# Late weight tiles of a dense layer: decode steps moved between the products and the low half, in the order of use

## The chip, the core and the metric

The kernel runs on one core of a Trainium2 chip. The metric is device time in microseconds (us), the median of several runs of the same compiled kernel. PE is TensorE, DVE is VectorE, ACT is ScalarE, POOL is GpSimd, SP is SyncE.

## The reference, cut to what matters

An attention-like recurrence gives x (3072 tokens of 384), a mixture of experts maps it to x again, and a gated dense layer ends the chain. Only the dense layer is touched:

```
g = x @ w_gate                     # 384 -> 1536
silu = g * (1.0 / (1.0 + np.exp(-g)))
val = x @ w_val                    # 384 -> 1536
return (silu * val @ w_out)        # 1536 -> 384
```

The three weight matrices of the dense layer reach the kernel as float64 bit patterns.

## The kernel before

**Two halves of a float.** Each fp32 operand of a matmul is split in a high part (a cast to fp32r on ACT) and a low part (source minus high part, on DVE); a product is three matmuls, high by high, high by low and low by high. `split` (L1431) issues the two instructions.

**The dense loop.** The tokens are in 8 blocks of 384, the hidden width in 12 parts f of 128. `seq` (L1568) runs block by block over the parts: 96 steps, numbered n, so steps 0 to 11 are the first block. A step issues `up2(j, f)` (L1521): 9 matmuls into the PSUM tile pg, 9 into pv, the sigmoid on ACT (L1532), two products on DVE (L1533 reads pg, L1534 reads pv, both write sg), then `split` of sg into the tiles hd, the high half by a cast on ACT (L1432), the low half on DVE (L1433). Two steps later `down2` (L1541) issues the 9 matmuls into po that read hd. There are two pg and two pv tiles, so the pg matmuls of step n+2 wait until L1533 of step n has read its pg. The engines run in the order in which the code issues, since the schedule is written out by hand.

**The weights.** Each part needs three weight tiles of 128 by 384: number m = 3f (gate), 3f+1 (val), 3f+2 (out), 36 in all. The first 30 (`NDEC`) are decoded from float64 during the mixture of experts and lie in fp32. In the dense loop `split_w2(n + 2)` (L1459) splits the three tiles of part n+2, ahead of `up2` of step n: three casts on ACT, three subtractions on DVE. That goes on through step 7.

**The six late tiles** (30 to 35, of parts 10 and 11) are decoded inside the first steps. `decode_parts` (L1252) gives five DVE instructions per tile: L1268 shifts, L1270 merges, L1272 takes the exponent, L1273 scales the low word, L1263 adds the two; after the last, `load_raw` (L1291) starts on POOL's queue the transfer of the tile three places on, into one of three rawd buffers. `decode_late` (L1450) adds a sixth part, `f_split`: cast on ACT and, right behind it, the subtraction on DVE that needs it. After `up2`, steps 0 to 7 take 5, 4, 5, 4, 5, 4, 5, 4 of these 36 parts (L1576 to 1582), tile by tile from 30 to 35. Parts 10 and 11 are used from steps 10 and 11 on, tiles 32 and 35 (out) first in steps 12 and 13.

Of the kernel before, what the change touches and what calls it, by code (L numbers as in the profile page):

```python
# [10 lines left out]
F32 = mybir.dt.float32  # L11
# [5 lines left out]
ALU = mybir.AluOpType  # L17
# [172 lines left out]
def tile_kernel(  # L190
# [8 lines left out]
    ve, sc, gp, pe, sy = nc.vector, nc.scalar, nc.gpsimd, nc.tensor, nc.sync  # L199
# [5 lines left out]
    P = 128  # L205
    NC_ = S // P
    NTILE = NT // P
    G3 = DM // P
    D2 = 2 * D
    KF1 = F1 // P  # L210
    KF2 = F2 // P
# [134 lines left out]
    for r in range(2):  # L346
# [7 lines left out]
        p=(1, WIDE), r=(1, WIDE), tw=(1, WIDE), ta=(1, WIDE), tr=(1, [P, CM, H, 2, D]),  # L354
# [793 lines left out]
    with tc.If(slow > 0):  # L1148
# [14 lines left out]
        with tc.For_i(0, S, TS) as t0:  # L1163
            tl = {}
            for nm, src in (("ar", a_re), ("ai", a_im), ("q", q), ("k", k)):
                t = slowp.tile([P, TS, D], F32, name="f" + nm)
# [8 lines left out]
            w = slowp.tile([P, TS, D], F32, name="fw")  # L1175
# [69 lines left out]
    NW = 3 * KF2  # L1245

    NDEC = NW - 6
    wls = ctx.enter_context(tc.tile_pool(name="wls", bufs=NDEC, reuse_waits="tile"))
    wf = [wls.tile([P, G3, P], F32, name="w") for m in range(NDEC)]
    raws = []  # L1250

    def decode_parts(m, w):  # L1252
        def raw():
            return raws[m % 3]

        def hw():
            return w().bitcast(I32)

        def hi():
            return raw()[:, :, :, 1]  # L1260

        def f_rest():
            ve.tensor_tensor(out=w(), in0=w(), in1=hi().bitcast(F32), op=ALU.add)  # L1263
            if m + 3 < (NDEC if m < NDEC else NW):
                load_raw(m + 3)

        return [
            lambda: ve.tensor_scalar(out=hw(), in0=hi(), scalar1=3, scalar2=0x3FFFFFFF, op0=ALU.logical_shift_left,  # L1268
                                     op1=ALU.bitwise_and),
            lambda: ve.scalar_tensor_tensor(out=hw(), in0=hi(), scalar=-0x40000000, in1=hw(), op0=ALU.bitwise_and,  # L1270
                                            op1=ALU.bitwise_or),
            lambda: ve.tensor_scalar(out=hi(), in0=hw(), scalar1=-0x00800000, scalar2=None, op0=ALU.bitwise_and),  # L1272
            lambda: ve.scalar_tensor_tensor(out=hi().bitcast(F32), in0=raw()[:, :, :, 0].bitcast(U32), scalar=2.0**-52,  # L1273
                                            in1=hi().bitcast(F32), op0=ALU.mult, op1=ALU.mult),
            f_rest,
        ]

    undone, parts = list(range(NDEC)), []

# [8 lines left out]
    decp = dec.enter_context(tc.tile_pool(name="decp", bufs=1, side="right", reuse_waits="tile"))  # L1288
    raws += [decp.tile([P, G3, P, 2], I32, name=f"raw{i}") for i in range(3)]

    def load_raw(m):  # L1291
        raw = raws[m % 3]
        f, i = divmod(m, 3)
        if i == 2:
            gp.dma_start(raw.rearrange("p g f t -> p (g f t)"), w2_out.bitcast(I32)[f * P : (f + 1) * P, :])
        else:
            src = (w2_gate, w2_val)[i].bitcast(I32)[:, f * 2 * P : (f + 1) * 2 * P]
            gp.dma_start(raw.rearrange("p g f t -> p g (f t)"), src.rearrange("(g p) f -> p g f", p=P))

    for m in range(3):  # L1300
        load_raw(m)
# [70 lines left out]
    def slot(s):  # L1372

        for f in range(KF1):
# [19 lines left out]
            step[0] += 1  # L1394
            while done[0] * STEPS < 5 * NDEC * step[0] and (parts or undone):
                if not parts:
# [21 lines left out]
    def den_pool(name, bufs, **kw):  # L1418
        return den.enter_context(tc.tile_pool(name=name, bufs=bufs, reuse_waits="tile", **kw))
# [3 lines left out]

    NEW0, NEW = 4, NW + NW - NDEC + 1
    dsoon = den_pool("dsoon", 1)
# [3 lines left out]
    xb, wd, wnew = {}, {}, [None]  # L1429

    def split(dst, src):  # L1431
        sc.copy(dst[0], src)  # L1432
        ve.tensor_tensor(out=dst[1], in0=src, in1=dst[0].bitcast(F32), op=ALU.subtract)  # L1433

    def prep_g(j, g):
        if j < len(BLKS):
            c, n = BLKS[j]
            xb[j] = xbs[j % 2]
            split([t[:, g, :n] for t in xb[j]], x2T[:, g, SLOT + c : SLOT + c + n])
# [3 lines left out]
    def new_hl():  # L1443
        n_hl[0] += 2
        return [(w0 if n < NEW0 else wnew[0] if n < NEW else wls).tile([P, G3, P], F32R, name="w")
                for n in (n_hl[0] - 2, n_hl[0] - 1)]

    late, late_parts = {}, []

    def decode_late(m):  # L1450
        w = latep.tile([P, G3, P], F32, name="wl")

        def f_split():
            late[m] = new_hl()
            split(late[m], w)

        return decode_parts(m, lambda: w) + [f_split]

    def split_w2(f, n_m=3):  # L1459
        wd.setdefault(f, [])  # L1460
        for m in range(3 * f + len(wd[f]), 3 * f + n_m):
            if m < NDEC:
                hl = new_hl()
                split(hl, wf[m])
            else:
                hl = late.pop(m)
            wd[f].append(hl if m % 3 < 2 else [t.rearrange("p g f -> p (g f)") for t in hl])

    soon_parts = [lambda g=g: prep_g(0, g) for g in range(G3)] + [lambda m=m: split_w2(0, m) for m in (1, 2)]
    slot(NSURE - 1)  # L1470
    assert not undone and not parts
# [34 lines left out]
    latep = den_pool("latep", 2)  # L1506
    raws[:] = [rawp.tile([P, G3, P, 2], I32, name=f"rawd{i}") for i in range(3)]
    for m in range(NDEC, NDEC + 3):
        load_raw(m)
# [8 lines left out]

    hd = {}

    def up2(j, f):  # L1521
        n_ = BLKS[j][1]
        ps = []
        for w, nm in zip(wd[f][:2], "gv"):
            p_ = dp_u.tile([P, BLK], F32, name="p" + nm)[:, :n_]
            xh, xl = xb[j]
            terms = [(a, xh, g) for g in range(G3) for a in w] + [(w[0], xl, g) for g in range(G3)]
            for n, (a, x, g) in enumerate(terms):
                pe.matmul(p_, a[:, g, :], x[:, g, :n_], start=(n == 0), stop=(n == 3 * G3 - 1))  # L1529
            ps.append(p_)  # L1530
        sg = dtwo.tile([P, BLK], F32, name="sg")[:, :n_]
        sc.activation(out=sg, in_=ps[0], func=AF.Sigmoid)  # L1532
        ve.tensor_tensor(out=sg, in0=sg, in1=ps[0], op=ALU.mult)  # L1533
        ve.tensor_tensor(out=sg, in0=sg, in1=ps[1], op=ALU.mult)  # L1534
        hl = [dthr.tile([P, BLK], F32R, name=f"hd{i}")[:, :n_] for i in range(2)]
        split(hl, sg)
        hd[j, f] = hl

    po = {}

    def down2(j, f, ts=range(BLK // P)):  # L1541
        hh, hl = hd[j, f]
        oh_, ol_ = wd[f][2]
        if f == 0:
            po[j] = [dp_o.tile([P, BLK], F32, name=f"po{t}") for t in range(BLKS[j][1] // P)]
        for t in ts:
            p_ = po[j][t]
            sl = slice(t * P, (t + 1) * P)
            for i, (h, w) in enumerate(((hh, oh_), (hh, ol_), (hl, oh_))):
                pe.matmul(p_[:, :DM], h[:, sl], w, start=(f == 0 and i == 0), stop=(f == KF2 - 1 and i == 2))  # L1550

    def write(j, ts=range(BLK // P)):
        for t in ts:
            p_ = po[j][t]
            o = dfou.tile([P, DM], F32, name="o")
            sc.copy(o, p_[:, :DM])  # L1556
            i = BLKS[j][0] // P + t
            d = gp.indirect_dma_start(out=out, out_offset=bass.IndirectOffsetOnAxis(ap=idu[:, i : i + 1], axis=0),  # L1558
                                      in_=o, in_offset=None)
            gp.memset(pause, 0.0)  # L1560

            tc.declare_no_dep(d.ins, group="out", reason="each token number occurs once")
            tc.add_to_no_dep_group("out", d.ins)

    split_w2(0)
    split_w2(1)
    late_done = []
    seq = [(j, f) for j in range(len(BLKS)) for f in range(KF2)]  # L1568
    for n, (j, f) in enumerate(seq):
        if f == KF2 - 2:  # L1570
            for g in range(G3):
                prep_g(j + 1, g)
        if n + 2 < KF2:
            split_w2(n + 2)
        up2(j, f)
        if n < KF2 - 3:  # L1576
            todo_late = -(-6 * (NW - NDEC) * (n + 1) // (KF2 - 4))
            while len(late_done) < min(todo_late, 6 * (NW - NDEC)):
                if not late_parts:
                    late_parts.extend(decode_late(NDEC + len(late_done) // 6))  # L1580
                late_parts.pop(0)()
                late_done.append(n)
        if n == KF2 // 2:
            ve.tensor_copy(idu, idf)

        if 1 < n < len(seq) - 1:
            jp, fp = seq[n - 2]
            down2(jp, fp)
            if fp == KF2 - 1:
                write(jp)  # L1590

    down2(*seq[-3])
    for t in range(BLK // P):
        for jp, fp in seq[-2:]:
            down2(jp, fp, (t,))
        write(len(BLKS) - 1, (t,))
# [34 lines left out]
```

## Time and profile before

| | |
|---|---|
| median of 3 runs | 947.86 us (947.84 to 947.98) |
| the profiled execution's own time | 950.28 us |
| its span, first to last instruction | 948.6 us |
| busy: PE, DVE, ACT, POOL | 904.9, 594.7, 448.9, 120.6 us |
| granted TensorE clock, mean of the span | 0.983 of full speed |

The dense loop begins at 481 us of the span and runs to its end. Times in the rows below count from the start of the span. A matmul of 128 by 384 shows as about 338 ns busy, but the matmuls overlap each other; the time from the first matmul of one step to the first of the next is what counts.

### The profile page before, as it was taken

To read this page: it belongs to the slowest core of one execution; us is meant where nothing else is said; L and a number is where in the kernel's file an instruction comes from. 1 tells how busy PE (TensorE), PEld (TensorE's weight loads), DVE (VectorE), ACT (ScalarE), POOL (GpSimd) and SP (SyncE) were. 2 spreads that over 40 slices of the span, in tenths; PEclk is the share of its full clock that TensorE was granted. 3 is DMA by queue.
4 is the path that set the end of the run, shared out by engine and by line. 5 is a ranking of instruction groups with operands and counts; after the bars stand their busy time and mean duration, and the time that the engine had idled before them with its cause. 6 is when DMAs were issued, how large, how long until landed. Compare 5 with 4: busy or idle time off the path is not lost. (4 is left out here: it accounts for less than half of the span.)

```text
span 948.6 us, 15710 instructions
## 1 busy us (share of the span) xinstructions
PE 904.9 (95%) x5980; PEld 868.9 (92%) x5980; DVE 594.7 (63%) x1147; ACT 448.9 (47%) x775; POOL 120.6 (13%) x210
## 2 busy tenths in 40 slices
PE   2789999999999999999998999999999999999997
PEld 1578889888998999999988899999999999999997
DVE  6999999988666888798778733334343343434332
ACT  6899887788645554545444322222222232222221
POOL 1112423322120101110010010100101000010101
PEclk9789999999998999999999999999999999999999
DMA  9999775683015574432121000000000000000000
GB/s 167 160 185 186 129 135 120 150 196 95 35 60 89 107 178 126 93 80 65 51 68 34 1 26 1 26 1 1 26 1 26 1 9 17 1 26 1 26 1 26
DMA packets 155646, 64.57 MB, mean 68 GB/s; under 512 B 135540, under 2 KB 150188, under 8 KB 155564
## 3 DMA queue, kind: packets, MB, share of 16 engines
q1 hardware_dynamic: 147564, 39.82, 22.8%
q0 software_dynamic: 8000, 23.69, 9.5%
q8 instruction: 48, 0.79, 0.4%
q14 instruction: 34, 0.28, 0.1%
HBM read 67.86 MB, written 14.37 MB: 87 GB/s over the span
## 5 line engine op out<-in xcount | busy, mean ns | idle before, releaser
L1529 PE MATMUL pg<-xb,w 128*128 128x384 f32 x864 | 167.6, 338 | 7.4 <-DVE sg L1533 6.1
L1529 PE MATMUL pv<-xb,w 128*128 128x384 f32 x864 | 167.6, 339 | 0.0
L1550 PE MATMUL po<-w,hd 128*128 128x384 f32 x864 | 165.7, 337 | 0.0
L1529 PEld LDWEIGHTS pg<-xb,w 128*128 128x128 f32 x864 | 152.2, 188 | 9.7 <-DVE sg L1533 8.1
L1533 DVE TENSOR_TENSOR sg<-sg,pg 128x384 f32<-128x384 f32 x96 | 53.1, 553 | 163.9 <-ACT sg L1532 163.9
L1529 PEld LDWEIGHTS pv<-xb,w 128*128 128x128 f32 x864 | 153.5, 191 | 0.0
L1550 PEld LDWEIGHTS po<-w,hd 128*128 128x128 f32 x864 | 151.6, 188 | 0.0
L1432 ACT CAST hd<-sg 128x384 fp32r<-128x384 f32 x96 | 49.3, 513 | 160.7 <-DVE sg L1534 160.7
L1532 ACT ACTIVATE sg<-pg 128x384 f32<-128x384 f32 x96 | 47.2, 491 | 161.6 <-PE pg L1529 161.6
L1433 DVE TENSOR_TENSOR hd<-sg,hd 128x384 fp32r<-128x384 f32 x96 | 53.5, 558 | 55.6 <-ACT hd L1432 51.6
L1534 DVE TENSOR_TENSOR sg<-sg,pv 128x384 f32<-128x384 f32 x96 | 53.2, 554 | 36.5 <-PE pv L1529 35.1
L1558 POOL DMA_INDIRECT out_dram<-o,idu x24 | 23.3, 972 | 408.9 <-ACT o L1556 405.8
L991 ACT ACTIVATE hh<-banks 128x396 fp32r<-128x396 f32 x64 | 32.1, 502 | 84.0 <-PE banks L988 80.5
L988 PE MATMUL banks<-xh,w1h 128*128 128x396 f32 x192 | 67.6, 352 | 1.6 <-DVEq L1238 1.6
L988 PE MATMUL banks<-xh,w1l 128*128 128x396 f32 x192 | 66.8, 348 | 0.0
L995 DVE SCALAR_TENSOR_TENSOR hl<-banks,hh 128x396 fp32r<-128x396 f32 x64 | 36.3, 567 | 34.0 <-ACT hh L991 33.6
L668 PE MATMUL banks<-tQ,tK 96*128 96x128 f32 x384 | 51.3, 279 | 0.0
L668 PEld LDWEIGHTS banks<-tQ,tK 96*128 96x128 f32 x384 | 46.5, 191 | 2.7 <-issue 1.4
L1002 PE MATMUL banks<-hh,w2l 128*128 128x396 f32 x192 | 47.7, 343 | 0.0
L1002 PE MATMUL banks<-hh,w2h 128*128 128x396 f32 x192 | 47.7, 343 | 0.0
L1002 PE MATMUL banks<-hl,w2h 128*128 128x396 f32 x192 | 47.7, 343 | 0.0
L988 PE MATMUL banks<-xl,w1h 128*128 128x396 f32 x192 | 45.9, 348 | 0.0
(217 smaller groups left out, 1533.7 us busy)
## 6 DMA issues: line engine op xcount, KB each, us to landing
st<-in_moe_w_dram SPq DMA_DIRECT2D x64, 384.0 KB
xrows<-zero SPq DMA_DIRECT2D x8, 597.1 KB
xg<-xrows SPq DMA_DIRECT2D x8, 597.1 KB
ar<-in_a_re_dram SPq DMA_DIRECT2D x24, 192.0 KB
ai<-in_a_im_dram SPq DMA_DIRECT2D x24, 192.0 KB
q<-in_q_dram SPq DMA_DIRECT2D x24, 192.0 KB
k<-in_k_dram SPq DMA_DIRECT2D x24, 192.0 KB
v<-in_v_dram SPq DMA_DIRECT2D x24, 192.0 KB
```

What stands on the lines that cost most here:

```text
L668: pe.matmul(plan[ap][:, i * P : (i + 1) * P], plan[kt][:, i, :], plan[qt][:, i, :], start=True, stop=True)
L988: pe.matmul(ps[:, :SLOT], a[:, g, o : o + P], x[:, g, :], start=(n == 0), stop=(n == 3 * G3 - 1))
L991: sc.activation(out=hidden(s, f)[0], in_=ps[:, :SLOT], func=AF.Relu)
L995: ve.scalar_tensor_tensor(out=hl, in0=ps[:, :SLOT], scalar=0.0, in1=hh.bitcast(F32), op0=ALU.max, op1=ALU.subtract)
L1002: pe.matmul(pds[:, g, :SLOT], w[:, f % 2, g * P : (g + 1) * P], x, start=(f == 0 and term == 0), stop=(f == KF1 - 1 and term == 2))
L1432: sc.copy(dst[0], src)
L1433: ve.tensor_tensor(out=dst[1], in0=src, in1=dst[0].bitcast(F32), op=ALU.subtract)
L1529: pe.matmul(p_, a[:, g, :], x[:, g, :n_], start=(n == 0), stop=(n == 3 * G3 - 1))
L1532: sc.activation(out=sg, in_=ps[0], func=AF.Sigmoid)
L1533: ve.tensor_tensor(out=sg, in0=sg, in1=ps[0], op=ALU.mult)
L1534: ve.tensor_tensor(out=sg, in0=sg, in1=ps[1], op=ALU.mult)
L1550: pe.matmul(p_[:, :DM], h[:, sl], w, start=(f == 0 and i == 0), stop=(f == KF2 - 1 and i == 2))
```

## The change

The decode parts of the late tiles are no longer issued behind `up2` but inside it, through a new argument `between`: behind the cast of the high half of hd and ahead of the subtraction that makes its low half. Steps 0 to 7 take three parts each, steps 8 and 9 six each (`N_LATE`; step 10 finds none left). The order of tiles becomes 30, 31, 33, 34, 32, 35 (`TURN_W`), for the transfers too. The sixth part of a tile is taken apart: its cast on ACT goes with the fifth part, its subtraction on DVE becomes the second part of the next tile.

```
+    TURN_W = list(range(NDEC)) + [NW - 6, NW - 5, NW - 3, NW - 2, NW - 4, NW - 1]
...
     def decode_late(m):
-        w = latep.tile([P, G3, P], F32, name="wl")
-
-        def f_split():
+        w = []
+
+        def f_hi():
             late[m] = new_hl()
-            split(late[m], w)
-
-        return decode_parts(m, lambda: w) + [f_split]
+            sc.copy(late[m][0], w[0])
+
+        def f_lo():
+            ve.tensor_tensor(out=late[m][1], in0=w[0], in1=late[m][0].bitcast(F32), op=ALU.subtract)
+
+        parts = decode_parts(m, lambda: w[0])
+        first, last = parts[0], parts[-1]
+        begin = lambda: (w.append(latep.tile([P, G3, P], F32, name="wl")), first())
+        return [begin] + parts[1:-1] + [lambda: (last(), f_hi())], f_lo
...
-    def up2(j, f):
+    def up2(j, f, between=lambda: None):
...
         ve.tensor_tensor(out=sg, in0=sg, in1=ps[1], op=ALU.mult)
         hl = [dthr.tile([P, BLK], F32R, name=f"hd{i}")[:, :n_] for i in range(2)]
-        split(hl, sg)
+        sc.copy(hl[0], sg)
+
+        between()
+        ve.tensor_tensor(out=hl[1], in0=sg, in1=hl[0].bitcast(F32), op=ALU.subtract)
         hd[j, f] = hl
...
-    late_done = []
+
+    for m in TURN_W[NDEC:]:
+        ps_, lo = decode_late(m)
+        if late_parts:
+            ps_.insert(1, late_parts.pop())
+        late_parts += ps_ + [lo]
+    N_LATE = [3] * (KF2 - 4) + [6] * 3 + [0]
+    assert sum(N_LATE) >= len(late_parts)
+
+    def decode_some(n):
+        def f():
+            for part in late_parts[: N_LATE[n]]:
+                part()
+            del late_parts[: N_LATE[n]]
+
+        return f
+
...
-        up2(j, f)
-        if n < KF2 - 3:
-            todo_late = -(-6 * (NW - NDEC) * (n + 1) // (KF2 - 4))
-            while len(late_done) < min(todo_late, 6 * (NW - NDEC)):
-                if not late_parts:
-                    late_parts.extend(decode_late(NDEC + len(late_done) // 6))
-                late_parts.pop(0)()
-                late_done.append(n)
+        up2(j, f, decode_some(n) if j == 0 else lambda: None)
```

The rest of the diff lets `load_raw` and the rawd buffers go by the place in `TURN_W` instead of the tile's number, and lets `up2` and `down2` fetch a part's weights by `w_of`. For the first 30 tiles place and number are the same.

## Rows read from the trace of the kernel before

**Rows 1.** Stretches: length, busy us of each engine (instructions), granted PE clock, DMA share, GB/s.
```profile
core 0: us, PE busy (x) PEld busy (x) DVE busy (x) ACT busy (x) POOL busy (x), PEclk, DMA share, GB/s
487.38:535.78 48.40, 42.25 (x217) 40.29 (x217) 39.47 (x83) 19.44 (x45) 2.05 (x3) 0.93 0.08 25
504.84:511.20 6.36, 6.36 (x27) 6.31 (x28) 4.98 (x11) 2.65 (x6) 0.56 (x1) 0.73 0.07 28
529.42:535.78 6.36, 6.36 (x27) 6.36 (x28) 4.35 (x9) 2.23 (x5) 0.00 (x0) 0.73 0.01 3
540.48:573.32 32.84, 32.84 (x190) 32.84 (x190) 12.27 (x23) 8.69 (x18) 3.34 (x6) 1.00 0.05 18
```

**Rows 2.** Waits, 487 to 536 us: who waited for whom, us, times, longest.
```profile
PE pg L1529 <- DVE sg L1533: 6.1, 6, 1.9
DVE hd L1433 <- ACT hd L1432: 5.2, 9, 0.6
DVE w L1433 <- ACT w L1432: 2.4, 4, 0.6
```

**Rows 3.** Chain that ended last, 491 to 506 us: start, us, what.
```profile
492.20 0.47 DVE sg L1533
...
492.76 0.56 DVE sg L1534
...
493.35 0.52 ACT hd L1432
...
493.90 0.56 DVE hd L1433
494.46 0.47 DVE w L1433
494.93 0.28 DVE wl L1268
...
495.23 0.57 DVE wl L1270
...
495.83 0.36 DVE rawd L1272
496.19 1.40 DVE w L1433 x3
497.59 0.47 DVE sg L1533
...
499.85 0.48 DVE rawd L1273
...
500.36 0.57 DVE wl L1263
...
500.95 0.52 ACT w L1432
...
501.49 0.56 DVE w L1433
...
504.32 0.47 DVE sg L1533
```

**Rows 4.** Order of time on DVE, steps 0 and 1: start, us, instruction, idle before.
```profile
485.99 0.55 DVE L1533 TENSOR_TENSOR sg<-sg,pg 128x384 f32<-128x384 f32 x1 [0.92 <-ACT sg L1532]
...
489.64 0.56 DVE L1273 SCALAR_TENSOR_TENSOR rawd<-rawd 128x384 f32<-128x384 uint32 x1
...
490.71 1.49 DVE L1433 TENSOR_TENSOR w<-w 128x384 fp32r<-128x384 f32 x3
492.11 0.55 DVE L1533 TENSOR_TENSOR sg<-sg,pg 128x384 f32<-128x384 f32 x1
```

**Rows 5.** Stretches of 1 us while the first late tiles land, columns as in rows 1.
```profile
485.00:486.00 1.00, 1.00 (x8) 1.00 (x7) 0.09 (x2) 0.95 (x2) 0.00 (x0) 1.00 1.00 338
487.00:488.00 1.00, 1.00 (x8) 1.00 (x7) 0.42 (x2) 0.76 (x2) 0.00 (x0) 1.00 0.00 0
```

**Rows 6.** Order of time on PE, the two longest waits of the first block.
```profile
504.84 2.00 PE L1529 MATMUL pg<-xb,w 128*128 128x384 f32 x9 [1.77 <-DVE sg L1533]
...
529.42 2.58 PE L1529 MATMUL pg<-xb,w 128*128 128x384 f32 x9 [1.86 <-DVE sg L1533]
```

More of the change, by code (lines that the diff above doesn't have):

```diff
@@ L1252, in decode_parts @@
     def decode_parts(m, w):
+        at = TURN_W.index(m)
         def raw():
-            return raws[m % 3]
+            return raws[at % 3]
         def hw():
@@ L1263, in f_rest @@
             ve.tensor_tensor(out=w(), in0=w(), in1=hi().bitcast(F32), op=ALU.add)
-            if m + 3 < (NDEC if m < NDEC else NW):
-                load_raw(m + 3)
+            if at + 3 < (NDEC if at < NDEC else NW):
+                load_raw(at + 3)
         return [
@@ L1289, in tile_kernel, with load_raw @@
     raws += [decp.tile([P, G3, P, 2], I32, name=f"raw{i}") for i in range(3)]
-    def load_raw(m):
-        raw = raws[m % 3]
-        f, i = divmod(m, 3)
+    def load_raw(at):
+        raw = raws[at % 3]
+        f, i = divmod(TURN_W[at], 3)
         if i == 2:
@@ L1450, in decode_late, with w_of @@
     def decode_late(m):
-        w = latep.tile([P, G3, P], F32, name="wl")
-        def f_split():
+        w = []
+        def f_hi():
             late[m] = new_hl()
-            split(late[m], w)
-        return decode_parts(m, lambda: w) + [f_split]
+            sc.copy(late[m][0], w[0])
[5 more added lines that the diff above has]
+        return [begin] + parts[1:-1] + [lambda: (last(), f_hi())], f_lo
     def split_w2(f, n_m=3):
         wd.setdefault(f, [])
[L1461 to L1467, printed above, removed]
+        for m in range(3 * f + len(wd[f]), min(3 * f + n_m, NDEC)):
+            hl = new_hl()
+            split(hl, wf[m])
+            wd[f].append(hl)
+    def w_of(f, i):
+        hl = wd[f][i] if 3 * f + i < NDEC else late[3 * f + i]
+        return hl if i < 2 else [t.rearrange("p g f -> p (g f)") for t in hl]
     soon_parts = [lambda g=g: prep_g(0, g) for g in range(G3)] + [lambda m=m: split_w2(0, m) for m in (1, 2)]
@@ L1519, in tile_kernel @@
     hd = {}
-    def up2(j, f):
+    def up2(j, f, between=lambda: None):
         n_ = BLKS[j][1]
         ps = []
-        for w, nm in zip(wd[f][:2], "gv"):
+        for w, nm in zip((w_of(f, 0), w_of(f, 1)), "gv"):
             p_ = dp_u.tile([P, BLK], F32, name="p" + nm)[:, :n_]
@@ L1542, in down2 @@
         hh, hl = hd[j, f]
-        oh_, ol_ = wd[f][2]
+        oh_, ol_ = w_of(f, 2)
         if f == 0:
```

## The prediction

> **What bounds the kernel now.** The page's shares of busy time say TensorE, and for the whole span that is right, so I went to the stretches first, cut at the first matmul of a step, to see where TensorE is not fed [rows 1]. From step 11 on the reader sees 7 whole steps in 32.84 us with TensorE busy throughout and a clock of 1.00: 32.84 / 7 = 4.69 us a step, and VectorE works 12.27 of the 32.84 us. The 8 steps 2 to 9 take 48.40 us, 6.05 each, with TensorE busy 42.25. At the later pace they would take 8 x 4.69 = 37.52 us; the excess is **10.88 us**, and it is all that a better order of these steps can give back. Steps 0 and 1, which have no po matmuls, run without a gap, and steps 10 on are at full pace already.
>
> Next come the waits, to see what ends last [rows 2]: pg of a step waits 6.1 us in six places for L1533, the product that frees the PSUM tile it writes. Two steps at a lower clock add 2 x (6.36 - 4.69) = 3.3 us [rows 1]; the remaining 1.5 lies in the matmuls' ends, which are modelled and reach into the gaps. So VectorE sets the pace. Its busy time in the stretch is 39.47 us, short of 48.40, but it also waits 5.2 us in nine places for the cast of hd and 2.4 us in four for the cast of a late tile: 39.47 + 5.2 + 2.4 = 47.1, nearly all of it.
>
> Third, the chain, which gives VectorE's cycle from one L1533 to the next [rows 3]. From 492.20 to 497.59 it is 5.39 us, and from there to 504.32 it is 6.73. Read downward: two products, a stand for ACT's cast of hd, the low half of hd, some decode parts, three subtractions of split_w2 at 1.40 together, and the next product.
>
> **The change part by part.** *Fewer parts a step.* Three instead of four or five; the rest goes to steps 8 and 9, which have no split_w2. There VectorE saves 1.40 us of subtractions [rows 3] and takes three more parts, about 1.5 us, so those cycles stay as long as the others.
>
> *Parts under the cast of hd.* The low half used to start 0.55 us after the cast's start (493.35 to 493.90, [rows 3]), with VectorE standing. Three parts last longer than that, so the cast is covered and 0.55 us a step goes. Had the cover gone (step 10, with no parts left) it would cost the same 0.55, where TensorE's 4.69 hides it.
>
> *The late tile's subtraction one part later.* Its stand behind the cast, 500.95 to 501.49, is 0.54 us on a tile [rows 3] and is covered by the next tile's L1268. Only the last tile, in step 9, has nothing between; VectorE has slack there.
>
> *The cycles that result.* The parts fall into two kinds of steps. The even ones hold low half, L1270, L1272: the cycle of 5.39 without the stand (0.55) and without L1268 (0.30, 494.93 to 495.23) is **4.54**. The odd ones hold L1273, L1263, L1268: 6.73 less 0.55, less 0.54, less the late low half 0.56 (501.49 to 502.05), less L1270, which I price at its 0.57, is **4.51** [rows 3]. In the odd ones the late cast now stands on ACT ahead of the three casts of split_w2 and the next sigmoid, and waits there for L1263. Cast plus the first cast of split_w2 take about 0.54 + 0.52 = 1.06 us from L1263's end, in which VectorE has L1268 and the low half of hd, 0.28 + 0.56 = 0.84 [rows 3]; the subtractions then start some 0.2 late. The trace has no row of this queue, so the bounds are 0 (casts keep ahead) and 0.54 (the whole late cast is in front): 4.51 to 5.05, and I take 4.7, nearer the overlap that the chain shows. The mean of 4.54 and 4.7 is 4.62 us, under TensorE's 4.69. **The bound passes to TensorE**, by a narrow 0.07 us a step.
>
> *The start.* Step 0 goes from L1533 at 485.99 to the next at 492.11, 6.12 us [rows 4]. Without 0.55 of stand and without L1273 and L1263 (489.64 to 490.71, 1.07) it is 4.50: L1533 of step 1 starts at 490.49 and ends at 491.04. TensorE, from 487.38, wants its PSUM tile at 487.38 + 4.69 = 492.07. VectorE therefore enters the stretch with 1.03 us in hand, and loses it nowhere at 4.62 against 4.69.
>
> *Low half of hd three parts later.* About 1.4 us on VectorE, in steps 8 and 9 about 2.9. Its first reader is po two steps later, behind pg and pv: for step 1 that is po of step 3 at about 492.07 + 3.13 = 495.2, and the low half is done about 2.9 us after 490.49 (the cycle up to the subtractions), at 493.4. Nothing, and in steps 8 and 9 VectorE runs further ahead. sg has two buffers, so its next writer is two steps off too.
>
> *Transfers.* The first three are tiles 30, 31, 33 instead of 30, 31, 32, and three more follow at the ends of the first three tiles, on a POOL queue that has nothing else in the block; SP's queue is not passed. The first part, L1268 of step 0, now comes about 1.1 us earlier, near 487.1. The transfers run at 338 GB/s in 485 to 486 us and nothing moves from 487 on [rows 5]: it finds its tile, with little to spare (bounds 0 and about 1 us, which the 1.03 in hand would take up; I take 0). Later tiles have several steps to land. The order by use costs nothing: tile 34's low half comes in step 8, for step 11; the last in step 9, for step 13.
>
> *The clock.* Where pg waited 1.77 and 1.86 us [rows 6], the granted clock of the step is 0.73, a mix of 1.2 and 2.4 GHz, and the step takes 6.36 us [rows 1]. These drops came after gaps, and without gaps the clock is 1.00 for 32.84 us. They are inside the 10.88. The first cost nothing by itself, as VectorE was as late.
>
> **Sum.** 10.88 us off the execution shown: its own time 950.28 becomes 939.40. The median stands 2.42 us below that execution (947.86), so I forecast 947.86 - 10.88 = **937.0 us**.
>
> **The rivals.** *A, VectorE still sets the pace.* At the odd cycles' upper bound the mean is (4.54 + 5.05) / 2 = 4.80, 0.11 over TensorE's; 8 steps lose 0.9, the 1.03 in hand nearly covers it. Gaps that stay, though, can bring a clock drop, and a step with one takes 6.36 - 4.69 = 1.67 longer [rows 1]. One or two drops and up to 1 us of gaps: 1.7 to 4.3 us less gain, 938.7 to 941.3 us. For it: the thin margin. Against it: odd and even cycles alternate and two PSUM tiles even them out.
>
> The Trainium skill (VectorE: DVE Perf Modes, The DRAIN you can't avoid) has a rule that speaks for A: the next VectorE instruction does not start until the pipe of the one before is empty, chained or not. By the rule the three subtractions would take 3 x 0.56 = 1.68 and not 1.40, the cycles near 4.9, and the time about 938 to 939; the trace of before disagrees, with three in 1.40 to 1.49 us where one takes 0.56 [rows 3, 4].
>
> *B, no change.* Something that the waits don't name, such as the sigmoid behind ACT's casts, holds pg as long as before: 946 to 949.8 us. Against it: L1533 follows the subtractions directly in the chain, with no stand for ACT [rows 3].
>
> *C, slower: a decode part meets a tile that has not landed.* VectorE takes instructions in order; the parts now stand ahead of the low half of hd, of the subtractions and of the next products, so a late tile stops pg two steps on. Place: L1268 of step 0. Price: each us that the tile lands after about 488 is a us of the whole; from about 12 us late (the 10.88 and the 1 in hand) the kernel is slower than before, say 950 to 952 us. Against it: all bytes have moved by 487 [rows 5].
>
> **How the numbers follow.** The forecast, with TensorE unbroken within half a us or so, gets 0.72 (936.2 to 938.5: if the second clock drop, about 1.3 us that VectorE did not hide, is missing in most runs, the gain is 9.6 and the time 938.3). A gets 0.21, B 0.04, C 0.03. The range goes from 936.2 through most of A, to 940.8. About 0.2%, 1.9 us, is what a measurement of this kernel can tell from no change; forecast and A lie beyond it, so faster is 0.93, same 0.04, slower 0.03.
>
> **What would show it.** Right: pg in steps 2 to 9 starts every 4.69 us and its wait for L1533 falls from 6.1 us to under 1; the wait of hd's low half for the cast falls from 5.2 us to nearly nothing in steps 0 to 9; the clock stays at 1.00 from 481 us on; step 10 begins near 525 instead of 535.78. A shows as pg waits in every second step, with split_w2's subtractions waiting for ACT in odd steps. C shows as L1268 waiting for a transfer. The forecast is wrong if steps 2 to 9 still take over 5.2 us each, or if the stretch shrinks and the time doesn't.

## The result and the profile after

The changed kernel takes **939.38 us**, the median of 4 runs (938.66 to 939.46), against 947.92 for before in the same comparison (4 runs): a ratio of 0.990, interval 0.9887 to 0.9912, which is 8.3 to 10.7 us. By the medians it is 8.5 us faster, by the means of the same runs 9.3, since one of the four runs of before took 950.26 us. It is 2.4 us slower than the 937.0 forecast. In a second comparison the medians differ by 9.1 us (below).

The profiled execution took 938.66 us, its span is 936.9. Its dense loop begins at 480.21 us, 0.79 earlier than in before. Stretches of the kernel after, cut at the first matmul of steps 2, 10, 12 and 19 (columns as in rows 1):

```profile
core 0: us, PE busy (x) PEld busy (x) DVE busy (x) ACT busy (x) POOL busy (x), PEclk, DMA share, GB/s
486.58:524.12 37.54, 37.54 (x217) 37.54 (x217) 35.24 (x77) 18.83 (x44) 1.86 (x3) 1.00 0.10 33
524.12:533.50 9.38, 9.38 (x55) 9.38 (x55) 7.67 (x17) 3.98 (x10) 0.00 (x0) 1.00 0.00 0
533.50:566.34 32.84, 32.84 (x190) 32.84 (x190) 12.99 (x25) 8.69 (x18) 3.34 (x6) 1.00 0.05 19
```

The first row answers to the first of [rows 1]: the 8 steps 2 to 9 take 37.54 us instead of 48.40, which is 8 x 4.69, TensorE's own pace; TensorE is busy throughout and the clock is 1.00. VectorE is busy 35.24 of 37.54 us, 94%, so its margin is thin. Steps 10 and 11 and the next block run at the same pace.

The waits from 486.58 to 528.82 us, those that answer to [rows 2]:

```profile
ACT hd L1547 <- DVE sg L1545: 17.0, 10, 2.3
...
ACT w L1459 <- DVE wl L1267: 6.3, 6, 2.0
DVE w L1437 <- ACT w L1436: 0.8, 3, 0.3
DVE sg L1544 <- ACT sg L1543: 0.5, 2, 0.2
```

No line has PE waiting for the product (L1544 is the old L1533), and none has hd's low half (L1550) waiting for its cast. The waits that are left are ACT's and POOL's, off the path that ended last, 0.5 us of VectorE for the sigmoid in steps 8 and 9, and 0.8 us of split_w2's subtractions behind ACT's casts, the queue for which the trace of before had no row. The chain that ended last holds nothing but PE there:

```profile
491.43 1.57 PE pg L1540 x9
493.00 1.56 PE pv L1540 x9
494.56 1.57 PE po L1564 x9
496.12 1.57 PE pg L1540 x9
```

Two of VectorE's cycles, from the order of time on VectorE and ACT (start, us, instruction, idle before), to be read beside [rows 3]:

```profile
489.46 0.55 DVE L1544 TENSOR_TENSOR sg<-sg,pg 128x384 f32<-128x384 f32 x1
...
490.58 0.55 DVE L1277 SCALAR_TENSOR_TENSOR rawd<-rawd 128x384 f32<-128x384 uint32 x1
...
491.17 0.56 DVE L1267 TENSOR_TENSOR wl<-wl,rawd 128x384 f32<-128x384 f32 x1
...
491.64 0.35 DVE L1272 TENSOR_SCALAR wl<-rawd 128x384 int32<-128x384 int32 x1
491.82 0.52 ACT L1459 CAST w<-wl 128x384 fp32r<-128x384 f32 x1 [0.60 <-DVE wl L1267]
491.91 0.55 DVE L1550 TENSOR_TENSOR hd<-sg,hd 128x384 fp32r<-128x384 f32 x1
...
492.78 1.50 DVE L1437 TENSOR_TENSOR w<-w 128x384 fp32r<-128x384 f32 x3 [0.31 <-ACT w L1436]
...
494.19 0.55 DVE L1544 TENSOR_TENSOR sg<-sg,pg 128x384 f32<-128x384 f32 x1
494.84 0.55 DVE L1545 TENSOR_TENSOR sg<-sg,pv 128x384 f32<-128x384 f32 x1
495.31 0.55 DVE L1462 TENSOR_TENSOR w<-wl,w 128x384 fp32r<-128x384 f32 x1
...
496.64 0.55 DVE L1550 TENSOR_TENSOR hd<-sg,hd 128x384 fp32r<-128x384 f32 x1
...
497.11 1.49 DVE L1437 TENSOR_TENSOR w<-w 128x384 fp32r<-128x384 f32 x3
...
498.52 0.55 DVE L1544 TENSOR_TENSOR sg<-sg,pg 128x384 f32<-128x384 f32 x1
```

The odd cycle, 489.46 to 494.19, is 4.73 us, the even one to 498.52 is 4.33. In the odd one the low half of hd starts with no idle time before it, and the subtractions of split_w2 (L1437) stand idle for 0.31 us, since the late cast (L1459) has gone ahead of theirs on ACT. They start 0.87 us after the low half of hd, in the even cycle 0.47.

### The profile page after: what moved, and what is told of

Read it like the earlier page. It is cut to its first block, busy times and chain, and to the rows that moved or that the text cites. A ratio compares the mean times of both kernels' runs of the same rounds, so it can differ in the third digit from the quotient of the medians.

```text
span 936.9 us, 15712 instructions
## 1 busy us (share of the span) xinstructions
PE 897.2 (96%) x5980; PEld 864.3 (92%) x5980; DVE 593.1 (63%) x1147; ACT 448.5 (48%) x775; POOL 121.1 (13%) x210
## 5 line engine op out<-in xcount | busy, mean ns | idle before, releaser
L1540 PE MATMUL pv<-xb,w 128*128 128x384 f32 x864 | 165.4, 336 | 0.0
L1544 DVE TENSOR_TENSOR sg<-sg,pg 128x384 f32<-128x384 f32 x96 | 53.2, 554 | 161.2 <-ACT sg L1543 161.2
L1540 PEld LDWEIGHTS pv<-xb,w 128*128 128x128 f32 x864 | 151.2, 188 | 0.0
L1550 DVE TENSOR_TENSOR hd<-sg,hd 128x384 fp32r<-128x384 f32 x96 | 53.5, 558 | 49.8 <-ACT hd L1547 49.8
L1545 DVE TENSOR_TENSOR sg<-sg,pv 128x384 f32<-128x384 f32 x96 | 53.2, 555 | 36.4 <-PE pv L1540 35.0
L494 PE MATMUL banks<-sx,tri 128*128 128x384 f32 x48 | 22.2, 582 | 24.8 <-DVE sx L469 24.7
```

Source lines behind the costliest of these rows:

```text
L1550: ve.tensor_tensor(out=hl[1], in0=sg, in1=hl[0].bitcast(F32), op=ALU.subtract)
```

## The experiments

**The changed kernel again.** No edit.

> The changed kernel a second time, beside before on one chip. Theory: the gain is the 10.9 us of steps 2 to 9, seen through a scatter of about 1 us that lies ahead of the dense loop; with more runs the medians differ by 9.5 to 11 us and the trace again has 4.69 us for each of steps 2 to 9. Rival: ordinary runs of before hold less than 10.9 us of excess in those steps, and the medians differ by 8.5 as at first.

Measured: 939.32 us (4 runs) against 948.39 (9 runs), ratio 0.9906 (0.9891 to 0.9921), 9.1 us; the trace has 37.54 us for steps 2 to 9 again. The stretch repeats to the hundredth, and the medians differ by less than it. The theory's 9.5 to 11 us was missed, though the interval, 7.5 to 10.3 us, does not shut out its lower part; the rival has a point.

**Fewer parts a step, nothing else.**

```
-        if n + 2 < KF2:
+        if n + 2 < KF2 - 2:
             split_w2(n + 2)
         up2(j, f)
-        if n < KF2 - 3:
-            todo_late = -(-6 * (NW - NDEC) * (n + 1) // (KF2 - 4))
+        if n < KF2 - 2:
+            todo_late = 3 * (n + 1) if n < KF2 - 4 else 24 + 6 * (n - 7)
...
+        if KF2 - 2 <= n + 2 < KF2:
+            split_w2(n + 2)
```

`split_w2` of parts 10 and 11 only picks up tiles that are already decoded; it is moved behind the decode and issues nothing itself.

> Before, with three parts a step in steps 0 to 7 and six in steps 8 and 9, still behind the low half of hd, tiles 30 to 35 in the old order and the late cast and subtraction together. Theory: both the number of parts and the stands behind ACT count. VectorE's cycle becomes 5.39 - 0.47 = 4.92 us and 6.73 - 0.86 = 5.87 us in turn, mean 5.4 against TensorE's 4.69: 8 x 0.7 less 1 us in hand, 4.6 us over the changed kernel, plus clock drops of up to 1.7 us each: 943 to 947 us. Rival: the number of parts is what matters alone: as the changed kernel, 939.4 us.

Measured: 947.93 us (11 runs) against 948.98 (21 runs), ratio 0.9984 (0.9975 to 0.9993), 0.9 us above the range that was expected. Order of time on VectorE in that kernel, steps 6 to 8 (L1533 and its neighbours as in before):

```profile
518.24 0.54 DVE L1533 TENSOR_TENSOR sg<-sg,pg 128x384 f32<-128x384 f32 x1
...
520.02 0.56 DVE L1433 TENSOR_TENSOR hd<-sg,hd 128x384 fp32r<-128x384 f32 x1 [0.58 <-ACT hd L1432]
...
523.24 0.55 DVE L1533 TENSOR_TENSOR sg<-sg,pg 128x384 f32<-128x384 f32 x1
...
533.07 0.56 DVE L1433 TENSOR_TENSOR w<-wl,w 128x384 fp32r<-128x384 f32 x1 [0.58 <-ACT w L1432]
533.55 0.55 DVE L1533 TENSOR_TENSOR sg<-sg,pg 128x384 f32<-128x384 f32 x1
```

The cycles from step 0 to step 5 are 4.93, 5.93, 4.93, 5.86 and 4.93 us, as expected (4.92 and 5.87); in steps 6 to 8 the two stands are still there. What the expectation left out comes later. VectorE enters step 8 with 0.4 us in hand (L1533 ends at 528.25, pg of step 10 begins at 528.64); in the changed kernel that is 3.7 us (520.40 and 524.12). With six parts and both stands its cycle there is still 5.85 us, from 527.70 to 533.55. Its waits from 528 to 546 us show where it is paid:

```profile
PE pg L1529 <- DVE sg L1533: 3.0, 2, 2.3
```

Steps 10 and 11 take 5.51 and 7.25 us, by their first pg matmuls at 528.64, 534.15 and 541.40. The excess over TensorE's pace is 3.9 us in steps 2 to 9 and 3.4 in steps 10 and 11, 7.3 us together, where before has 10.9 with clock drops and 9.4 without (below). The number of parts alone is worth about 1 us in the medians, 0.7 to 2.4 by the ratio; the rival falls.

**The old numbers of parts.**

```
-    N_LATE = [3] * (KF2 - 4) + [6] * 3 + [0]
+    N_LATE = [5, 4] * 4 + [0] * 4
```

> The changed kernel with the old numbers of parts, 5, 4, 5, 4, 5, 4, 5, 4 in steps 0 to 7 and none after. Theory: the cycle is 4.62 + 1.5 x 0.49 = 5.35 us, 8 x 0.66 less 1 us in hand, 4.3 us over the changed kernel, plus clock drops of up to 1.7 us each: 942.5 to 947 us. Rival: placing the parts under the cast is what matters alone: 939.4 us.

Measured: 943.41 us (5 runs), ratio 0.9947 (0.9933 to 0.996): 4.0 us over the changed kernel, expected 4.3. TensorE's order of time has gaps again, with the product L1544 as the releaser (first pg matmuls of steps 6, 7 and 8):

```profile
507.03 1.85 PE L1540 MATMUL pg<-xb,w 128*128 128x384 f32 x9
...
513.17 1.83 PE L1540 MATMUL pg<-xb,w 128*128 128x384 f32 x9 [0.99 <-DVE sg L1544]
517.96 1.73 PE L1540 MATMUL pg<-xb,w 128*128 128x384 f32 x9
```

Steps 2 to 9 take 42.20 us (486.42 to 528.62). VectorE's cycles from step 0 to step 7 take 5.41 us on average, expected 5.35. So the place is worth more than the number, and neither alone brings the cycle under 4.69. This kernel keeps the late subtraction apart from its cast and the new order of tiles; the place without these two was not run.

**One part more a step.**

```
-    N_LATE = [3] * (KF2 - 4) + [6] * 3 + [0]
+    N_LATE = [4] * 9 + [0] * 3
```

> The changed kernel with four parts in each of steps 0 to 8 instead of three in 0 to 7 and six in 8 and 9. Theory: VectorE's cycle is 4.62 + 0.49 = 5.11 us, above TensorE's 4.69, so the margin is gone: 8 x 0.42 less 1 us in hand, 2.4 us over the changed kernel, with small gaps and hardly a clock drop: 940.8 to 943 us, pg waits for L1544 in most steps. Rival: VectorE has room for a part more: 939.4 us.

Measured: 941.16 us (5 runs), 1.8 over the changed kernel on the same chip. The stretch takes 39.23 us, with a clock of 1.00, and VectorE's cycles from step 1 to step 7 take (521.21 - 490.87) / 6 = 5.06 us on average:

```profile
487.39:526.62 39.23, 38.92 (x217) 37.35 (x217) 36.39 (x80) 18.79 (x43) 1.86 (x3) 1.00 0.10 31
```

```profile
490.87 0.54 DVE L1544 TENSOR_TENSOR sg<-sg,pg 128x384 f32<-128x384 f32 x1
...
521.21 0.55 DVE L1544 TENSOR_TENSOR sg<-sg,pg 128x384 f32<-128x384 f32 x1
```

That is 1.7 over 37.54, expected 2.4. Not eight cycles lie over TensorE's pace but these six, by 0.37 us each, and VectorE had 0.66 us in hand at pg of step 3, not 1 (L1544 of step 1 ended at 491.41, pg of step 3 began at 492.08): 6 x 0.37 - 0.66 is about 1.6. The cast of hd is still covered; a fourth part takes VectorE's cycle over TensorE's, and three is the number that fits.

**The late subtraction directly behind its cast.**

```
-        if late_parts:
-            ps_.insert(1, late_parts.pop())
```

> The changed kernel with the late tile's subtraction directly behind its cast, as the sixth part of its own tile, instead of one part later. Theory: every second cycle gets a stand of 0.54 us back: 5.3 and 4.37 us in turn, mean 4.85, 0.16 over TensorE's; 8 x 0.16 less 1 us in hand is 0.3 us, at most 1.5: 939.3 to 941 us. Rival: ACT's late cast comes so late that each stand shows whole: 3 to 4 us more.

Measured: 940.1 us (5 runs), 0.8 over the changed kernel (939.32), which is less than the scatter of either's runs. VectorE's cycles in steps 0 to 6 alternate between 4.26 and 5.20 us, expected 4.37 and 5.3. Its waits from 487 to 540 us:

```profile
DVE w L1462 <- ACT w L1459: 3.5, 6, 0.6
PE pg L1540 <- DVE sg L1544: 0.4, 1, 0.4
```

The stand of about 0.58 comes back on all six tiles. Steps 2 to 9 absorb it, at 4.69 each, and the margin is used up only at step 11, which takes 5.31 us (529.37 to 534.68). That is 0.6 us over TensorE's pace, so the trace bears most of the 0.8 out. Splitting the cast from the subtraction is the smallest piece of the change that is worth anything.

**The old order of tiles.**

```
-    TURN_W = list(range(NDEC)) + [NW - 6, NW - 5, NW - 3, NW - 2, NW - 4, NW - 1]
+    TURN_W = list(range(NW))
```

> The changed kernel with tiles and transfers in the old order 30 to 35. Theory: the order of use costs and brings nothing, as tile 34 is still done two steps ahead of its use: 939.4 us within 0.4, same trace in steps 2 to 9 (4.69 us each). Rival: the order is needed: TensorE waits in step 11 for tile 34, one us or more longer.

Measured: 939.27 us (4 runs) against 948.98, 9.7 us, ratio to before 0.9906 (0.9891 to 0.9921), and the same stretch:

```profile
486.37:523.91 37.54, 37.54 (x217) 37.54 (x217) 35.23 (x77) 18.84 (x44) 2.05 (x3) 1.00 0.11 33
```

The order of use is worth nothing here.

**Before again.** Five more traces of the unchanged kernel, without an edit, to find the 2.4 us between forecast and result.

> The unchanged kernel before, profiled a second time. Open: the profiled stretch shrank by the 10.88 us forecast, the medians by 8.5 only. Theory: the ordinary runs of before are shorter than the profiled one (948.6 us span) because they hold one clock drop fewer in the first block, about 1.3 to 1.7 us each; the runs then show a mean clock of 0.985 or more and times near 947.9, and the new trace, if it is such a run, a step 9 of about 4.9 us instead of 6.36. Rival: the first block is the same 48.4 us for steps 2 to 9 in every run, and the 2.4 us lie ahead of 481 us, in the attention and expert stages.

> One more look at before, for its time and the two parts of its trace, up to the first pg of step 2 and from there to step 10. Theory: steps 2 to 9 take 48.4 us again, whatever the time; what differs lies ahead of 487 us. Rival: a run near 947.9 us has fewer clock drops in steps 5 and 9 and takes 46.5 to 47 us for them.

> Three more looks at before (this is the first of them), to see what a run with a higher mean clock looks like: times of before fall from about 950.1 us at a mean clock of 0.985 or less to 948.0 at 0.990. Theory: a run at 0.987 or more has no clock drop in step 9, and steps 2 to 9 take about 47.0 us, as with the filled gaps. Rival: these steps take 48.4 us in every run, and the difference lies ahead of the first block, whose first pg then comes well before 480 us.

> The second of three looks at before. Theory: at a mean clock of 0.987 or more steps 2 to 9 take about 47.0 us. Rival: 48.4 us in every run, the difference lies ahead.

> The third of three looks at before. Theory: at a mean clock of 0.987 or more steps 2 to 9 take about 47.0 us. Rival: 48.4 us in every run, the difference lies ahead.

Measured: 949.78 us (11 runs, the profiled one 950.07), then single runs of 950.98, 949.36, 949.6 and 949.73. With the trace that the prediction was read from they make six traces of before, numbered here in the order of the runs. Steps 2 to 9 of the second trace:

```profile
487.12:535.56 48.44, 42.31 (x218) 40.32 (x217) 39.50 (x83) 19.48 (x45) 2.06 (x3) 0.93 0.08 25
```

Steps 2 to 9 of the fourth trace, its step 9, and PE's wait for the product from 487 to 536 us:

```profile
487.76:534.73 46.97, 39.51 (x218) 37.07 (x217) 38.64 (x81) 18.64 (x43) 2.06 (x3) 1.00 0.09 26
529.81:534.73 4.92, 4.92 (x28) 4.71 (x28) 3.52 (x7) 1.42 (x3) 0.00 (x0) 1.00 0.02 3
...
PE pg L1529 <- DVE sg L1533: 7.5, 7, 1.9
```

The fourth trace has no clock drop at all in this stretch: it takes 46.97 us, and the fifth takes 46.96. The third takes 48.45 and the sixth 48.43. Of six traces of before, four have both drops and two have neither, and the stretch is 48.4 or 47.0 us by that alone. Step 9 takes 4.92 us without the drop and 6.36 with it. Step 5 takes 6.26 and 6.36, and step 6 gives the 0.1 back (6.12 and 6.01): there VectorE was as late, as forecast.

Both explanations hold in part. The first pg of step 2 comes between 486.80 (the sixth trace) and 488.03 us (the third), so about 1.2 us of scatter lies ahead; and a run without drops has 9.4 us of excess instead of 10.9. Across the 60 runs of before that were made for these experiments, on three chips, the times go with the mean clock: 950.2 us on average at 0.985 or less (28 runs), 948.0 at 0.990 (7 runs). What the clock of each run without a trace did in this stretch can't be seen.

**TensorE kept busy through the two longest gaps of before.**

```
             down2(jp, fp)
+            if n in (4, 8):
+                pf = dp_o.tile([P, BLK], F32, name="pf")
+                for _ in range(9):
+                    pe.matmul(pf, wd[0][0][0][:, 0, :], xb[0][0][:, 0, :BLK], start=True, stop=True)
```

> Before, with nine matmuls more behind po of steps 4 and 8, into an unused PSUM tile that nobody reads, so that TensorE is busy through the two longest waits (1.77 and 1.86 us in the rows of before). Theory: the clock stays at 1.00 in steps 5 and 9, since its drops follow those two gaps; step 9 falls from 6.36 to about 5.0 us and step 5 stays at 6.3, as VectorE is as late there without a drop: 1.3 to 1.5 us less than before. What of the 10.9 us the clock alone is worth is then that much. Rival: the drops have another cause, the two steps stay at 6.36 us, same time as before. Second rival: the drops go in the trace but ordinary runs never had the one that counts: median as before.

Measured: 949.46 us (11 runs) against 949.93 (15 runs), ratio 0.9994 (0.9985 to 1.0003), no difference that these runs can tell. The trace:

```profile
487.06:534.06 47.00, 42.61 (x235) 40.10 (x235) 38.64 (x81) 18.68 (x43) 2.05 (x3) 1.00 0.09 26
504.57:510.83 6.26, 4.96 (x27) 4.63 (x27) 4.93 (x10) 2.65 (x6) 0.56 (x1) 1.00 0.08 12
529.15:534.06 4.91, 4.91 (x27) 4.63 (x28) 3.52 (x7) 1.42 (x3) 0.00 (x0) 1.00 0.00 0
```

It has no drop, 47.00 us for the stretch, and step 9 at 4.91: the 1.4 us expected. The median moved by 0.5, as it would if many of the runs of before lack the drop anyway, which is the second rival's case. Two traces of before without drops and gaps as long as ever show that the fill is not needed for a clock of 1.00, so this one trace does not show that the fill kept it there. The mean clock of the 11 runs was 0.987 on average, that of the 15 runs of before 0.986, which fits a fill that helps in some runs and is too little to show it.

## Why the prediction was right, and where it was off

**The bound.** Right: VectorE set the pace of steps 2 to 9 through L1533, and the bound passed to TensorE. The stretch gave back 48.40 - 37.54 = 10.86 us of the forecast 10.88. The waits fell away with it, and the experiments that put a part of the work or of the stands back lost about what the cycles say. The profiled executions differ by 950.28 - 938.66 = 11.62 us: 10.86 here and 0.79 ahead of the dense loop.

**The cycles.** I forecast 4.54 and 4.7 us, measured 4.33 and 4.73 in the cycles shown. The even one came out 0.2 shorter because VectorE starts an instruction that does not need the one before it ahead of that one's end, 0.47 us after the start of one of 0.55, and the prices that I read from the chain left that out. The order of time on VectorE in before shows the starts:

```profile
492.76 0.55 DVE L1534 TENSOR_TENSOR sg<-sg,pv 128x384 f32<-128x384 f32 x1
493.90 0.56 DVE L1433 TENSOR_TENSOR hd<-sg,hd 128x384 fp32r<-128x384 f32 x1 [0.58 <-ACT hd L1432]
...
494.84 0.36 DVE L1268 TENSOR_SCALAR wl<-rawd 128x384 int32<-128x384 int32 x1
495.23 0.56 DVE L1270 SCALAR_TENSOR_TENSOR wl<-rawd,wl 128x384 int32<-128x384 int32 x1
```

From L1534 to the low half of hd it was 1.14 us; now a subtraction that needs neither follows L1545 after 0.47 (494.84 to 495.31). That is a gain of 0.67, priced at 0.55. L1268 held VectorE for 0.39 (494.84 to 495.23), priced at 0.30. In the odd cycle luck helped: its floor, forecast at 4.51, was too long in the same way, and the late cast cost more than the 0.2 that I added. The subtractions came 0.40 later than in the even cycle (0.87 against 0.47 behind the low half), so that without it the odd cycle would be 4.33, as the even one; the two misses nearly cancel. The mean of the two cycles is 4.53, forecast 4.62, so the margin was 0.16 us and not 0.07. The start: VectorE had 1.26 us in hand at pg of step 3 (L1544 of step 1 ended at 490.01, pg of step 3 began at 491.27), forecast 1.03.

**Parts of the change.** With the old numbers of parts 4.0 us of the gain are missing, with the new numbers alone most of it; the separate subtraction is worth 0.6 to 0.8, the order nothing. The hidden costs stayed hidden: hd's low half had no reader waiting on PE, and step 0's first decode part found its tile (L1272 at 486.33, 0.47 us after L1545's start, with no idle time before it). The forecast had VectorE's cycles in steps 8 and 9 as long as the others. The one of step 9 took 6.67 us (L1544 at 524.57 and 531.24), with the last tile's stand of 0.58 and three subtractions for the next block's x in it; the 3.7 us in hand hid that. The six parts of steps 8 and 9 were right for the changed kernel only, where VectorE enters them in time; in the kernel with the number alone they moved 3.4 us of waiting into steps 10 and 11.

**The rule of the Trainium skill** (VectorE: DVE Perf Modes, The DRAIN you can't avoid) that spoke for rival A was given there without its exception: the section goes on that "A next op that is not held starts earlier". The trace after goes with the exception, as that of before did: the three subtractions take 1.50 us together where one takes 0.55, and the cycles shown stayed under 4.9.

**Rivals.** A did not come: no gap stayed, and the odd and even cycles did even out. B and C did not come either. But 939.4 us lies above the 936.2 to 938.5 that the prediction kept for its own mechanism, among the times that it gave to A (938.7 to 941.3). That the whole range held the time is therefore in part luck.

**What was off** is the last step, "The median stands 2.42 us below that execution (947.86), so I forecast 947.86 - 10.88". It takes the excess of one profiled execution from the median of others. That execution had both clock drops and 48.40 us of stretch; two of six traces have 46.96 or 46.97. From such a run the change can take only 47.0 - 37.5 = 9.4 us, and that sum gives 938.4; the prediction had named this case as 9.6 us and 938.3. The remaining 1 us is of the size of the scatter ahead of step 2, 1.2 us between traces of the same kernel.

That the runs at 947.9 were runs without drops is likely, and not shown, as none of them has a trace here. An estimate from the six traces of before: from the first matmul of step 10 to the span's end they take 412.7 to 412.9 us, and the time is about 1.7 us over the span, so a run of 947.86 us comes to step 10 at about 533.3. With a stretch of 47.0 us its step 2 would begin at 486.3, with 48.4 at 484.9; the earliest in the traces is 486.80. So such a run would also have to begin early: the two traced runs without drops began step 2 at 487.76 and 487.99 and took 949.36 and 949.6 us, hardly less than the 949.73 of one with drops.

The split of the excess was off too. It put 6.1 us to waits, 3.3 to two clock drops and 1.5 to the matmuls' ends. Without drops PE waits 7.5 us for the product and the excess is 9.4, so both drops together add 1.4 to 1.5 and not 3.3: the drop in step 5 covers the wait of 1.31 us that step 6 has without it.

## What to carry to other kernels

Where two engines take turns on a shared buffer, write down the slower one's cycle from the chain and take out the stands one by one: work that nobody waits for soon, put between an instruction and the result it waits for on another engine, is free as long as the cycle stays under the other engine's. Check how near that is; here three parts fit and four did not. Before an excess read from one profiled execution is taken from a median, look at a second profile: time at a lower clock can be in one execution and not in the next.

## What the runs showed of the hardware that was not expected

The same kernel with the same gaps of 1.8 us on TensorE, at the same places, ran the following step at a granted clock of 0.73 in four traces and at 1.00 in two. In the kernel with fewer parts a step a longer gap, 2.30 us ahead of step 12, was followed by a step at 1.00 (order of time on PE, then the step's stretch):

```profile
541.40 1.85 PE L1529 MATMUL pg<-xb,w 128*128 128x384 f32 x9 [2.30 <-DVE sg L1533]
...
541.40:546.21 4.81, 4.81 (x27) 4.81 (x28) 3.40 (x7) 1.81 (x4) 0.00 (x0) 1.00 0.00 0
```

So a gap of this length did not decide by itself whether the clock fell; what did is open. A drop cost 1.4 us where TensorE was the one waited for (step 9, 6.36 against 4.92) and nothing where VectorE was as late (step 5, 6.36 against 6.26, and step 6, 6.01 against 6.12).
